# Second MLP product by Strassen's seven block products for pairs of token tiles

## The chip, the core and the metric

The kernel runs on one core of one Trainium2 chip. The time of a run is the device time of that core in microseconds. A run before the change and a run after it are compared as ratios of such times on the same chip.

## The reference, cut to what matters

```python
q_n, k_n = rmsnorm(q, g_q), rmsnorm(k, g_k)            # (8, 12, 448, 64) each
attn = softmax(q_n @ k_n.T / 8)                        # per batch and head, 448 x 448
x = (attn @ v).transpose(0, 2, 1, 3).reshape(8, 448, 768)
h = x.transpose(0, 2, 1) @ U @ V                       # mixes tokens through rank 32
u = x + h.transpose(0, 2, 1)
out = u + np.maximum(u @ w_ch1, 0.0) @ w_ch2           # 768 -> 3072 -> 768
```

Inputs and output are 32-bit floats. Attention of 12 heads gives x for each of 8 batches, a low-rank mixer over the 448 tokens gives u, and a two-layer MLP with a residual gives the output. The MLP's two products have 8 x 448 x 768 x 3072 multiplications each; they are most of the arithmetic.

## The kernel before, in words

All matmul operands are bf16, sums are 32-bit in PSUM. The 3584 tokens of the eight batches are cut into 28 tiles of 128 tokens. Since 448 is three and a half tiles, two batches share one tile: an even batch has three whole tiles and half a shared one, an odd batch the other half and three whole ones (`OFFS`, `tiles` of 3 for even and 4 for odd batches).

**Stages.** `head()` works off a hand-written word list (`HEAD`) for the attention and mixer of batch 0. Then the loop at the end of the kernel runs `mlp(b)` for b = 0 to 7, and `weave` puts the pieces of `attention(b + 1)` and `mixing(b + 1)` between the matmuls of `mlp(b)`: `mlp` is a generator which yields after six matmuls the number of columns they streamed, and `weave` takes from it until the columns done reach the share that is due to the next piece. Attention is spread over 72% of an MLP's columns and mixing over the next 13.5% (for batch 0's MLP, 58.5% and 13.5%). The schedule is manual: the order in which the Python code issues is the order on each engine, and each engine works off its own queue in that order. Semaphores are derived from the accesses to tiles.

**The MLP.** `mlp(b)` (L389) has two halves. The first product takes the batch's tiles together: for each of 24 blocks of 128 hidden columns, six matmuls with a 128 x 128 block of `w1b` as weights stream 384 (even batch) or 512 (odd batch) columns of the transposed u (tile `uA` or `uB`) into one PSUM bank `ph` (L399). ScalarE (L402) or VectorE (L404) writes its ReLU to `hT`. The second product takes tile by tile and half by half of the 768 output columns: 24 matmuls with a 128 x 128 block of `hT` as weights stream 384 columns of `w2b` into one PSUM bank `po` (L423), and VectorE adds the residual tile (L427) into `osb`, which SyncE's queue stores. That makes 28 x 2 x 24 = 1344 matmuls of 384 columns, the last 24 of them cut into 48 of 192.

**Attention.** For each pair of heads p (48 in all, `t` is two pairs): SyncE's queue loads q, k (`load`, L187) and v (`load_v`, L192; two buffers `vt`); GpSimd squares (L216), VectorE sums the squares (`reduce`, L219), ScalarE takes the inverse root (L224, L225), GpSimd scales (L230, tile `qkn`, three buffers), a DMA transposes (L263), ScalarE applies the gains (L268). From batch 2 on, at an even p both squares for two pairs of heads later are issued, and both sums at the odd p after it, so each sum stands about one pair of heads behind its squares. Scores (L281) go into banks `sc` or `sh`, ScalarE exponentiates them (L289), `products` (L296) multiplies with v, and `normalize` (L308 to L316) divides and writes x. GpSimd casts v (L202).

**Mixing.** `mix_t` and `mix_x` (L343 to L371) add the low-rank term to x in place, and `turn_u` (L373) has SyncE's queue transpose each tile to `uA` or `uB`.

**PSUM.** There are eight banks. The pool `ps_mm` has four of one bank each, which `ph`, `po`, `sh`, `o`, `pm`, `px` and `pt` take in turn; `ps_s` has two of two banks for `sc`.

## Time and profile before

| what | number |
|---|---|
| runs of the kernel before | 582.85, 584.38, 584.50 us (median 584.38) |
| the profiled execution, first to last instruction | 581.1 us |
| median of the runs less that span | 3.3 us |
| first product, matmuls of 384 and of 512 columns (L399) | 552 and 576 (24 more of 384 columns stand in `begin`, L547) |
| second product, matmuls of 384 and of 192 columns (L423) | 1320 and 48 |
| VectorE, ScalarE, GpSimd busy | 252.3, 268.5, 192.4 us |
| granted TensorE clock | 1.000 |

The page lists no time of its own for the profiled execution beside the span: what lies around the span is taken from the runs. In the profile's lines, L12 is line 12 of the kernel, PE is TensorE's matmuls, PEld its weight loads, DVE is VectorE, ACT ScalarE, POOL GpSimd and SP SyncE. A timeline line gives the start and the time from the first start to the last end, both in us, of a run of equal instructions. Matmuls overlap: the spacing from start to start, and not the duration of one, is what a matmul costs in a stream.

### The profile page before, as it was taken

To read this page: it belongs to the slowest core of one execution; us is meant where nothing else is said; L and a number is where in the kernel's file an instruction comes from. 1 tells how busy PE (TensorE), PEld (TensorE's weight loads), DVE (VectorE), ACT (ScalarE), POOL (GpSimd) and SP (SyncE) were. 2 spreads that over 40 slices of the span, in tenths; PEclk is the share of its full clock that TensorE was granted. 3 is DMA by queue.
4 is the path that set the end of the run, shared out by engine and by line. 5 is a ranking of instruction groups with operands and counts; after the bars stand their busy time and mean duration, and the time that the engine had idled before them with its cause. 6 is when DMAs were issued, how large, how long until landed. Compare 5 with 4: busy or idle time off the path is not lost.

```text
span 581.1 us, 11317 instructions
## 1 busy us (share of the span) xinstructions
PE 572.9 (99%) x4749; PEld 323.8 (56%) x4749; DVE 252.3 (43%) x565; ACT 268.5 (46%) x481; POOL 192.4 (33%) x147
## 2 busy tenths in 40 slices
PE   7999999999999999999999999999999999999997
PEld 3665665445655556545565566544565555654565
DVE  5967767233442447234152445524344152521111
ACT  6967541666306761366601874066730576112200
POOL 5956026453520553223550255405433030000000
PEclk9999999999999999999999999999999999999999
DMA  8999997845546146625154452762454310140021
GB/s 270 265 245 237 204 265 172 203 119 142 152 96 167 32 131 167 154 79 140 38 161 103 132 142 57 194 168 22 136 141 98 60 33 1 44 95 0 1 54 55
DMA packets 108275, 72.27 MB, mean 124 GB/s; under 512 B 56656, under 2 KB 104768, under 8 KB 108224
## 3 DMA queue, kind: packets, MB, share of 16 engines
q1 hardware_dynamic: 96544, 61.50, 41.2%
q0 software_dynamic: 11008, 9.44, 10.0%
q8 instruction: 37, 0.61, 0.4%
q10 hardware_dynamic: 672, 0.61, 0.4%
q14 instruction: 14, 0.11, 0.1%
HBM read 56.78 MB, written 11.01 MB: 117 GB/s over the span
## 4 chain that ended last, share of the span: by engine, by line
PE 93%; ACT 2%; DMA 2%; DVE 2%; SPq 0%; issue 0%
PE po L423 38%; PE ph L399 37%; PE o L296 7%; PE sc L281 4%; PE sh L281 3%; PE px L369 1%; ACT E L289 1%; DMA Uf<-in_moe_U_dram 1%; DMA qk<-in_k_dram 1%; PE bank L296 1%; PE sc L547 1%; ACT hT L402 1%; DVE qkn L230 1%; PE pm L343 1%; PE pt L245 0%; SPq L185 0%
## 5 line engine op out<-in xcount | busy, mean ns | idle before, releaser
L423 PE MATMUL po<-w2b,hT 128*128 128x384 bf16 (+1 forms) x1368 | 237.6, 323 | 0.0
L423 PEld LDWEIGHTS <-hT 128*128 128x128 bf16 x1368 | 128.4, 98 | 84.7 <-issue 7.0
L399 PEld LDWEIGHTS <-w1b 128*128 128x128 bf16 x1128 | 104.5, 98 | 103.1 <-issue 12.0
L230 POOL TENSOR_TENSOR qkn<-qk,rms 112x1024 bf16<-112x1024 f32 x36 | 68.4, 1901 | 221.4 <-issue 220.4
L399 PE MATMUL ph<-uB,w1b 128*128 128x512 bf16 x576 | 131.0, 379 | 0.0
L289 ACT ACTIVATE E<-sc 112x896 bf16<-112x896 f32 x138 | 123.8, 918 | 5.2 <-PE sc L281 2.5
L289 ACT ACTIVATE E<-sh 112x448 bf16<-112x448 f32 x108 | 52.8, 542 | 140.4 <-PE sh L281 140.3
L402 ACT ACTIVATE hT<-ph 128x512 bf16<-128x512 f32 (+1 forms) x122 | 66.7, 547 | 95.9 <-PE ph L399 95.7
L399 PE MATMUL ph<-uA,w1b 128*128 128x384 bf16 x552 | 98.6, 326 | 0.6 <-ACT E L289 0.5
L216 POOL TENSOR_TENSOR sq<-qk 112x1024 f32<-112x1024 f32 x42 | 78.9, 1893 | 50.8 <-DVE rec L308 23.2
L404 DVE TENSOR_SCALAR hT<-ph 128x384 bf16<-128x384 f32 (+1 forms) x66 | 41.0, 620 | 108.2 <-PE ph L399 108.0
L296 PEld LDWEIGHTS <-E 112*128 112x128 bf16 x1536 | 61.0, 98 | 15.0 <-issue 1.6
L296 PE MATMUL o<-va,E 112*128 112x65 bf16 x1344 | 56.8, 194 | 0.0
L308 DVE RECIPROCAL rec<-o 128x4 f32<-128x4 f32 x84 | 15.1, 180 | 89.5 <-PE o L296 89.1
L219 DVE TENSOR_REDUCE sums<-sq 112x16 f32<-112x1024 f32 x43 | 50.5, 1208 | 2.4 <-POOL sq L216 1.3
L281 PE MATMUL sc<-qkT 64*128 64x448 bf16 x268 | 39.3, 351 | 1.1 <-DVE qkT L252 0.8
L427 DVE TENSOR_TENSOR osb<-po,xe 128x384 f32<-128x384 f32 x32 | 17.8, 557 | 47.7 <-PE po L423 47.2
L281 PEld LDWEIGHTS <-qkT 64*128 64x128 bf16 (+1 forms) x384 | 15.5, 94 | 31.2 <-issue 19.8
L427 DVE TENSOR_TENSOR osb<-po,xo 128x384 f32<-128x384 f32 (+1 forms) x25 | 13.5, 539 | 42.3 <-PE po L423 42.3
L268 ACT ACTIVATE qkT<-qkT,gg 128x448 bf16<-128x448 bf16 x36 | 24.1, 668 | 2.7 <-DMA qkT<-qkn 2.7
L202 POOL CAST va<-vt 112x1024 bf16<-112x1024 f32 x23 | 23.9, 1041 | 1.8 <-DMA vt<-in_v_dram 1.8
L371 DVE TENSOR_TENSOR xe<-px,xe 128x384 bf16<-128x384 f32 x32 | 17.8, 555 | 15.0 <-PE px L369 10.5
(98 smaller groups left out, 262.2 us busy)
## 6 DMA issues: line engine op xcount, KB each, us to landing
qk<-in_q_dram SPq DMA_DIRECT2D x44, 256.0 KB, 4.3
qk<-in_k_dram SPq DMA_DIRECT2D x44, 256.0 KB, 4.7
vt<-in_v_dram SPq DMA_DIRECT2D x22, 512.0 KB, 5.9
w1b<-in_moe_w_ch_dram POOLq DMA_DIRECT2D x6, 768.0 KB, 21.5
w2b<-in_moe_w_ch_dram POOLq DMA_DIRECT2D x6, 768.0 KB, 34.0
out_dram<-osb SPq DMA_DIRECT2D x7, 336.0 KB, 3.4
out_dram<-osb SPq DMA_DIRECT2D x8, 288.0 KB, 2.9
out_dram<-osb SPq DMA_DIRECT2D x8, 240.0 KB, 2.8
```

The costliest lines, as they stand in the source:

```text
L216: nc.gpsimd.tensor_tensor(dst, src, src, OP.mult)
L219: nc.vector.tensor_reduce(rs_of(p, of=sums).rearrange("p (s h j) -> p s h j", s=2, h=2)[:, :, hs], sqs[p].rearrange("p (s h j d) -> p s h ...
L230: (nc.gpsimd if p >= 12 else nc.vector).tensor_tensor(qkns[p].rearrange("p j g d -> p g j d"), qk_of[t][0:SP, a].rearrange("p s h (j d) -> ...
L268: nc.scalar.activation(qT, qT, AF.Copy, scale=gg)
L281: nc.tensor.matmul(sc[hh][0:n, 0:S], flat[pp, c:c + n], blocks(p)[pp, :, 0], start=True, stop=True)
L289: nc.scalar.activation(dst, src, AF.Exp, scale=float(D) ** 0.5)
L296: nc.tensor.matmul(o[:, i, :], E[:, hh, c:c + P], va[:, hl, kc, :], start=(kc == 0), stop=(kc == NJ - 1))
L399: nc.tensor.matmul(ph, w1b[:, dc, hc * P:(hc + 1) * P], u[:, dc, :], start=(dc == 0), stop=(dc == KD - 1))
L402: nc.scalar.activation(hT[:, hc, 0:n], ph, AF.Relu)
L404: nc.vector.tensor_relu(hT[:, hc, 0:n], ph)
L423: nc.tensor.matmul(po, hT[:, hc, i * P:(i + 1) * P], w2b[:, half, hc, w0:w1], start=(hc == 0), stop=(hc == KH - 1))
L427: nc.vector.tensor_add(osb[:, cols], po, xt[i][:, cols])
```

## The change

Batch 0's three whole tiles go through both products as before (`mlp_first`, with `hT` cut to 384 columns). The shared tile 3 goes alone (`mlp_single`): 144 matmuls of 128 columns in the first product, 48 of 384 in the second. The other 24 tiles go as 12 pairs (`mlp_pair`). A pair's first product has 24 x 6 matmuls of 256 columns, two hidden blocks to a bank, with one ReLU of 512 elements for two blocks. Its second product is read as a 2 x 2 block product: the rows are the two token tiles, the inner blocks the even and the odd hidden blocks, the columns the two halves of the output. Instead of eight block products of 12 matmuls it has seven of 12 (84 matmuls of 384 columns), in Winograd's form of Strassen's scheme:

- combinations of the hidden values, for each pair of tiles: S1 and S2 on VectorE, S3 and S4 on GpSimd, each in three pieces of 128 x 512 bf16, S3 over A21 and S4 over A12 in place;
- combinations of the weights, once: T1, T2 and T4 (six pieces of 2304 elements, VectorE, in `mlp_single`), T3 over B12 in place (six pieces of 768, VectorE, in the first pair);
- three PSUM banks W, X and Y each take two products: W is read after the first by ScalarE (to `part`), X and Y by VectorE; the second product accumulates on what stands there. Z takes one;
- sums of the results: six additions from PSUM on VectorE, two in SBUF on GpSimd (384 and 768 elements wide).

For space, x lies in a ring of nine tiles `xr` and the transposed u in a ring of four `ur`; a transpose into a slot that is still to be read is held back until `have_read` is called. `opool` has two buffers for three, `qkn` two for three, `sq` one for two, `vt` one for two. So from batch 2 on the squares of pair p + 4 are issued at p and their sum at the end of the same p, and v is loaded at the odd p before its cast. Attention and mixing are woven up to named places: batch 2's attention over the single tile and the first pair's first product, and so on (`ends`).

```diff
-    opool = ctx.enter_context(tc.tile_pool(name="opool", bufs=3))
+    opool = ctx.enter_context(tc.tile_pool(name="opool", bufs=2))
...
-    hT = consts.tile([P, KH, 512], BF16, name="hT")
-    Uf = consts.tile([SP, NJ * rank], FP32, name="Uf")
-    Us = consts.tile([SP, NJ, rank], BF16, name="Us")
+    comb = consts.tile([P, 3, KH // 2, HALF], BF16, name="comb")
+    hT = consts.tile([P, KH * 384], BF16, name="hT")
+    h0 = hT.rearrange("p (k n) -> p k n", n=384)
+    h3 = hT[:, 0:KH * P].rearrange("p (k n) -> p k n", n=P)
+    hB = hT.rearrange("p (s k n) -> p s k n", s=6, n=P)
+    spare = hT.bitcast(FP32)
+    early = comb.rearrange("p s k n -> p (s k n)").bitcast(FP32)
+
+    def slot(i, n=1024):
+        return early[:, i * 1024:i * 1024 + n]
+
...
+    NX, NU = 9, 4
+    xr = consts.tile([P, NX, dm], BF16, name="xr")
+    ur = consts.tile([P, KD, NU * P], BF16, name="ur")
+    zero = xr[:, NX - 1]
...
-    vL = [consts.tile([P, HG, NJ * D], FP32, name=f"vt{i}") for i in range(2)]
+    vL = consts.tile([P, HG, NJ * D], FP32, name="vt")
+    part = consts.tile([P, HALF], FP32, name="part")
...
+        elif p < 16 and p not in sqs:
+            sqs[p] = slot(p % 4 if p > 5 else p)[0:SP]
         elif p not in sqs:
-            sqs[p] = norm.tile([SP, 2 * 2 * NJ * D], FP32, tag="sq", name="sq")
+            sqs[p] = norm.tile([SP, 2 * 2 * NJ * D], FP32, tag="sq", name="sq", bufs=1)
...
-        qkns[p] = norm.tile([SP, NJ, 4, D], BF16, tag="qkn", name="qkn", bufs=3)
+        qkns[p] = norm.tile([SP, NJ, 4, D], BF16, tag="qkn", name="qkn", bufs=2)
...
+    read, waiting = set(), []
+
+    def turn_u(t):
+        if t >= NU and t - NU not in read:
+            waiting.append(t)
+        else:
+            nc.sync.dma_start_transpose(out=u_of(t), in_=x_of(t))
+
+    def have_read(ts):
+        read.update(ts)
+        for t in [t for t in waiting if t - NU in read]:
+            waiting.remove(t)
+            turn_u(t)
...
+    def plain(po, left, half):
+        for hc in range(KH):
+            nc.tensor.matmul(po, left(hc), w2b[:, half, hc, :], start=(hc == 0), stop=(hc == KH - 1))
+            if hc % 6 == 5 and hc != KH - 1:
+                yield HALF
+
+    def mlp_single(t):
+        u = u_of(t)
+        for k in range(0, KH, 4):
+            ph = ps_mm.tile([P, 4, P], FP32, tag="mm", name="ph")
+            for j in range(4):
+                for dc in range(KD):
+                    nc.tensor.matmul(ph[:, j], w1b[:, dc, (k + j) * P:(k + j + 1) * P], u[:, dc, :],
+                                     start=(dc == 0), stop=(dc == KD - 1))
+                if j == 1:
+                    yield 2 * P
+            relu(h3[:, k:k + 4, :], ph, k % 3)
+            combine(k // 4)
+            yield 2 * P
+        have_read([t])
+        osb = new_osb()
+        for half in range(2):
+            cols = slice(half * HALF, (half + 1) * HALF)
+            po = ps_mm.tile([P, HALF], FP32, tag="mm", name="po")
+            yield from plain(po, lambda hc: h3[:, hc, :], half)
+            nc.vector.tensor_add(osb[:, cols], po, x_of(t)[:, cols])
+            yield HALF
+        put(t, osb)
...
+    w2v = w2b.rearrange("p l (k j) n -> p j l k n", j=2)
+    B11, B12, B21, B22 = w2v[:, 0, 0], w2v[:, 0, 1], w2v[:, 1, 0], w2v[:, 1, 1]
+    T1, T2, T4 = (comb[:, i] for i in range(3))
+    T3 = B12
+    A11, A21, A12, A22, S1, S2 = (hB[:, i] for i in range(6))
+    S3, S4 = A21, A12
+
+    def combine(i):
+        ks = slice(i % 2 * 6, i % 2 * 6 + 6)
+        for out, x, y in (((T1, B12, B11),), ((T2, B22, T1),), ((T4, B21, T2),))[i // 2]:
+            nc.vector.tensor_tensor(out[:, ks], x[:, ks], y[:, ks], OP.subtract)
+
+    def product(bank, left, right, start, cols=slice(0, HALF)):
+        for k in range(KH // 2):
+            nc.tensor.matmul(bank, left[:, k, :], right[:, k, cols], start=start and k == 0,
+                             stop=k == KH // 2 - 1, skip_group_check=not start)
+            if k == 5:
+                yield cols.stop - cols.start
+
+    def mlp_pair(g):
+        t0, u, last = 2 * g + 2, u_of(2 * g + 2, 2), 2 * g + 4 == 28
+        for k in range(KH // 2):
+            ph = ps_mm.tile([P, 4, P], FP32, tag="mm", name="ph")
+            for j in range(2):
+                hc, out = 2 * k + j, ph[:, 2 * j:2 * j + 2].rearrange("p a n -> p (a n)")
+                for dc in range(KD):
+                    nc.tensor.matmul(out, w1b[:, dc, hc * P:(hc + 1) * P], u[:, dc, :],
+                                     start=(dc == 0), stop=(dc == KD - 1))
+                if j == 0:
+                    yield 2 * P
+            relu(hB[:, 0:4, k, :], ph, k % 3)
+            if g == 1 and k % 2 == 0:
+                ks = slice(k, k + 2)
+                nc.vector.tensor_tensor(T3[:, ks], B22[:, ks], B12[:, ks], OP.subtract)
+            if k % 4 == 3:
+                ks = slice(k - 3, k + 1)
+                nc.vector.tensor_tensor(S1[:, ks], A21[:, ks], A22[:, ks], OP.add)
+                nc.vector.tensor_tensor(S2[:, ks], S1[:, ks], A11[:, ks], OP.subtract)
+                nc.gpsimd.tensor_tensor(S3[:, ks], A11[:, ks], A21[:, ks], OP.subtract)
+            yield 2 * P
+        have_read([t0, t0 + 1])
+        x0, x1 = x_of(t0), x_of(t0 + 1)
+        c0, c1 = slice(0, HALF), slice(HALF, dm)
+        osb0, osb1 = new_osb(), new_osb()
+
+        def bank():
+            return ps_mm.tile([P, HALF], FP32, tag="mm", name="po")
+
+        W = bank()
+        yield from product(W, A11, B11, True)
+        nc.scalar.copy(part, W)
+        yield HALF
+        Z = bank()
+        yield from product(Z, A22, T4, True)
+        nc.vector.tensor_tensor(osb1[:, c0], Z, x1[:, c0], OP.add)
+        yield HALF
+        yield from product(W, A12, B21, False)
+        nc.vector.tensor_tensor(osb0[:, c0], W, x0[:, c0], OP.add)
+        for k in range(0, KH // 2, 4):
+            ks = slice(k, k + 4)
+            nc.gpsimd.tensor_tensor(S4[:, ks], A12[:, ks], S2[:, ks], OP.subtract)
+        if last:
+            put(t0, osb0, c0)
+        yield HALF
+        X = bank()
+        yield from product(X, S2, T2, True)
+        nc.vector.tensor_tensor(osb0[:, c1], X, part, OP.add)
+        nc.gpsimd.tensor_tensor(osb0[:, c1], osb0[:, c1], x0[:, c1], OP.add)
+        yield HALF
+        Y = bank()
+        yield from product(Y, S1, T1, True)
+        nc.vector.tensor_tensor(osb1[:, c1], Y, x1[:, c1], OP.add)
+        yield HALF
+        yield from product(X, S3, T3, False)
+        nc.vector.tensor_tensor(part, X, part, OP.add)
+        both = osb1.rearrange("p (h n) -> p h n", h=2)
+        nc.gpsimd.tensor_tensor(both, both, part.rearrange("p n -> p () n").to_broadcast([P, 2, HALF]), OP.add)
+        put(t0 + 1, osb1)
+        yield HALF
+        parts = [slice(0, HALF // 2), slice(HALF // 2, HALF)] if last else [slice(0, HALF)]
+        for c in parts:
+            d = slice(HALF + c.start, HALF + c.stop)
+            yield from product(Y[:, c], S4, B22, False, c)
+            nc.vector.tensor_tensor(osb0[:, d], Y[:, c], osb0[:, d], OP.add)
+            if last:
+                put(t0, osb0, d, (nc.sync, nc.scalar))
+            yield c.stop - c.start
+        if not last:
+            put(t0, osb0)
...
-            if t + 2 < NT:
-                for a in range(2):
-                    if odd and p > 11 or p == 11 and a == 0:
-                        add(0, reduce, 2 * t + 4 + a if p > 11 else 12)
-                    elif not odd and not early:
-                        add(0, squares, 2 * t + 4 + a)
+            if p == 11:
+                add(0, reduce, 12)
+            elif t + 2 < NT and not early:
+                add(0, squares, p + 4)
...
-            if odd and p > 11 and t + 3 < NT:
-                add(0, load, t + 3)
-                add(0, load_v, t + 3)
+            if odd and p > 11:
+                if t + 3 < NT:
+                    add(0, load, t + 3)
+                if t + 2 < NT:
+                    add(0, load_v, t + 2)
             if not odd and t + 1 < NT:
                 add(0, cast_v, t + 1)
             run(p, 3)
+            if t + 2 < NT and not early:
+                add(0, reduce, p + 4)
             if early and odd and p < 11:
                 add(1, transposes, p + 1)
...
+        spans = [("first", KH * 384 + KH * HALF), ("single", KH * P + 8 * HALF)]
+        stages = [mlp_first(), mlp_single(3)]
+        for g in range(1, 13):
+            stages.append(mlp_pair(g))
+            spans += [(("ph", g), KH * 2 * P), (("po", g), 14 * HALF)]
+        begins, c = {}, 0
+        for key, n in spans:
+            begins[key] = (c, n)
...
+        ends = {2: ("po", 1), 3: ("po", 3), 4: ("ph", 5), 5: ("po", 6), 6: ("po", 8), 7: ("po", 10)}
+        for b, key in ends.items():
+            weave(fill, place(key, 0.05), attention(b))
+            weave(fill, place(key, 0.6), mixing(b))
```

## The prediction

> **What bounds the kernel now.** I read the page's first lines, then the chain of work that ended last, then the timeline of TensorE, then the groups of instructions by shape.
>
> ```profile
> span 581.1 us, 11317 instructions
> ...
> PE 572.9 (99%) x4749; PEld 323.8 (56%) x4749; DVE 252.3 (43%) x565; ACT 268.5 (46%) x481; POOL 192.4 (33%) x147
> ...
> PE   7999999999999999999999999999999999999997
> ...
> PEclk9999999999999999999999999999999999999999
> ```
>
> TensorE has work in every slice and its clock is whole (1.000 over the span). A busy PE need not be PE at its peak, so I look at spacings in the timeline (start, time from first start to last end, count):
>
> ```profile
> 25.63 0.33 PE L359 MATMUL bank<-shift,xe 128*128 128x128 bf16 x3
> ...
> 50.50 0.67 PE L296 MATMUL o<-va,E 112*128 112x65 bf16 x16
> ...
> 239.14 1.46 PE L399 MATMUL ph<-uB,w1b 128*128 128x512 bf16 x6
> ...
> 299.76 2.12 PE L423 MATMUL po<-w2b,hT 128*128 128x384 bf16 x12
> ```
>
> Take the duration of one (0.219, 0.194, 0.379, 0.326 us in the groups) off each and divide by the count less one: 55 ns for 128 columns, 32 ns for 65, 216 ns for 512, 163 ns for 384. The spacing grows with the columns, about 0.42 ns for each, and each of these matmuls loads weights of its own: weight loads hide at 32 ns. So TensorE's columns set the end, and 38% and 37% of the chain are L423 and L399, the two lines that change.
>
> Adding such spacings for all matmuls from the first ph of the loop on gives 523 us of the 539 between 38.6 and 577.9 us; the other 16 us are changes of shape (a session of scores starts some 0.1 us late and costs another 0.1) and short waits. The other engines' work hides almost wholly: the hardest stretch, the first product of batch 0's MLP (38.6 to 68.9, 30.3 us), holds 27.9 us of columns, 24.3 us of VectorE's work and 22.7 of ScalarE's by their rows.
>
> **What goes and comes on TensorE.**
>
> - Second product. Before: 1320 x 0.163 + 48 x 0.083 (192 columns: 0.163 less 192 x 0.42 ns) = 219.2 us. After: 144 (batch 0) + 48 (tile 3) + 12 x 84 = 1200, the last 12 cut in 24: 1188 x 0.163 + 24 x 0.083 = 195.6. **23.6 us go.**
> - First product. The columns stay; matmuls go from 1152 to 144 x 384, 144 x 128 and 1728 x 256. No row has 256: between 128 and 384 lies 109 ns, on the line through 384 and 512 lies 110. Before: 576 x 0.163 + 576 x 0.216 = 218.3. After: 23.5 + 7.9 + 1728 x 0.1095 = 220.6. **2.3 us come** (1.5 to 3.2 by the two ends).
>
> Net: 21.3 us less. The changed order shows all other matmuls unchanged in number.
>
> The Trainium skill speaks against the short matmuls: "TensorE: Matmul & The Clock Gate", section "Back-to-back issue gap", gives about 81 ns for each pair of weight load and matmul at 128 columns in a sustained stream. This trace has 55 ns there and 32 ns at 65 columns; by the page tile 3's first product would cost 3.7 us more.
>
> **What the other engines get.** Durations: VectorE's addition from PSUM to SBUF, 384 wide, 0.56 us (L427, L371). Its additions with both inputs bf16 in SBUF have no row. From above, the shortest 1024-wide 32-bit one with both in SBUF took 1.22 us (L230), less or plus 1.04 ns an element: 0.69 us for 512, 0.95 for 768, 2.55 for 2304. From below, a bf16 copy of 448 took 0.38 (L252), at 0.52 ns an element: 0.41, 0.55, 1.35. I take the lower ends, because the operands are 16-bit as in that copy. GpSimd by its rows (128: 0.40, 384: 0.83, 1024: 1.90): 1.05 for 512, 1.47 for 768.
>
> - VectorE: S1 and S2 72 x 0.41 = 30; T1, T2, T4 6 x 1.35 = 8; T3 6 x 0.55 = 3; 81 additions for 57, +13; x tiles that wrap in the ring, 24 more of 0.22, +5: 252 to about 311 us (340 by the upper ends).
> - GpSimd: per pair 6 x 1.05 + 0.83 + 1.47 = 8.6, x 12 = 103: 192 to 295 us.
> - ScalarE: 12 copies to `part`, 0.49 each: 268 to 274.
>
> None reaches TensorE's 550, so on the whole this is hidden. What can be seen are places:
>
> 1. **Tile 3 and the first pair's first product, with batch 2's attention.** TensorE's columns there are 41.8 us (31.6 of MLP, the rest attention and mixing); VectorE's work by its rows is 36 us at the lower ends, 47 at the upper, a share like that of the hardest stretch before (87%), but bunched: six T pieces come within 8 us of TensorE's work, and ReLUs, row sums and divisions queue behind them, whose banks TensorE then waits for. Nothing at best, 47 - 42 = 5 plus up to 8 for the port below at worst. I take 2.5, near that stretch's 30.3 - 27.9.
>
> 2. **Banks that are taken twice.** W, X and Y's second products wait for a reader of the first. Between lie 12 matmuls, 1.95 us, and attention pieces; the reader needs 0.49 to 0.56 plus what is ahead of it on ScalarE (an exponential, 0.92) or VectorE (a row sum 1.21, a division 0.76). Mostly in time. 36 such waits: 0 to 0.25 us each, 0 to 9; with batches woven through nine pairs I take 2.5. Two or three of the four banks are held then; `sh`, `o` and `px` share the rest.
>
> 3. **VectorE behind GpSimd.** The row sum of p + 4 waited for squares issued 10.5 us of TensorE's columns or more before; now 2.8 at least, 5.4 in the median, over 31 sums. GpSimd has 1.90 for the squares and up to 3.5 us ahead of them by its own list, and in three places a cast whose v was ordered only 3.5 to 6 us earlier (landing takes 5.9, behind four loads of q and k). A VectorE that stands holds ReLUs and divisions, and behind these stand banks. 0 to 0.5 us a sum, 0 to 15; I take 1.5, since backlogs reach that far in few places.
>
> 4. **The end.** The last product's two halves share bank Y; the second half waits for VectorE's 0.36 and its signals: +0.7. Before, they had two banks.
>
> On GpSimd S4 stands before the seventh product with 6.5 us of columns or more to spare for three pieces (3.2); S3 has 11. SyncE's queue: the transposes of u wait for tiles to be read, 8.5 us or more ahead of use against 2.9 for one; stores of a pair have 15 us before a buffer is asked for again. Loads issue as before, less double buffering of v. Where that cover goes, each pair would lose the excess, a microsecond or so. The head has the same words with two `qkn` buffers for three, every release issued before its next user: nothing, give or take 0.5.
>
> A row says VectorE and GpSimd get in each other's way. The shortest L230 on VectorE took 1.22 us; this one met a cast:
>
> ```profile
> 56.15 1.04 POOL L202 CAST va<-vt 112x1024 bf16<-112x1024 f32 x1 [1.01 <-DMA vt<-in_v_dram]
> ...
> 56.59 1.67 DVE L230 TENSOR_TENSOR qkn<-qk,rms 112x1024 bf16<-112x1024 f32 x1
> ```
>
> It ended 1.07 us after the cast, as if it had waited for it: +0.45. The 84 new VectorE additions with two SBUF inputs would meet GpSimd about half the time (295 of 570): 84 x 0.5 x 0.45 = 19 us on VectorE, in the bounds of places 1 and 3.
>
> The Trainium skill has this as a rule: "SBUF — State Buffer", section "Who interferes with whom", says such an instruction and a GpSimd instruction that reads SBUF exclude each other for their whole length. By it the loss per meeting could be a whole 1.90 instead of 0.45, and GpSimd's S3, issued just behind S1, could hold S2 up.
>
> **The sum.** 581.1 - 21.3 + 2.5 + 2.5 + 1.5 + 0.7 = 567.0 of span; with the 3.3 us between span and median, which I carry over, **570.3 us**.
>
> **Rivals.** A run within 0.3% of 584.4 (582.6 to 586.1) can't be told from no change.
>
> - *All of it hides*, as nearly all does now: 584.4 - 21.3 + 0.7 = 563.8. For it: shares of 87% cost little before. Against: the shortened distances.
> - *The places cost about double or triple* (2.5 + 2.5 + 1.5 becomes 13 to 19): 577 to 582.6. For it: the meetings on the port.
> - *GpSimd becomes the bound through VectorE's queue: slower.* Scales, squares, casts, S3, S4 and sums stand in one queue; at a row sum, 1.90 + 1.90 + 1.05 = 4.9 us of it against 2.8 of distance makes VectorE stand 2.1, of which a bank's slack takes about 1.2. With 31 sums at 0.9: 28 us, 570.3 - 1.5 + 28 = 597. It decides from 0.5 us a sum on, where the gain left (584.4 - 570.3 + 1.5 = 15.6) is eaten. Against it: in most places the queue is empty when squares come, and after batch 7's attention (60 us of TensorE) nothing of it is there.
> - *The gain is not there*: if 256 columns cost what a 384 does, 1728 x 0.054 = 93 us more. The rows from 65 to 512 columns lie on one line, so I give this next to nothing.
>
> **Chances.** Forecast (565 to 577) 0.60, all hides (below 565) 0.10, double or triple (577 to 582.6) 0.14, no change 0.05, slower 0.11. Faster 0.84, same 0.05, slower 0.11. The range 562 to 582 leaves out the last two and a little at each end.
>
> **What would show it.** Right: the group of 256 columns at 109 to 110 ns spacing; the 1188 of 384 columns in the second product at 163; PE in the nineties of every slice; VectorE near 311, GpSimd near 295. Place 1 shows as gaps on PE between about 90 and 140 us, place 2 as waits of PE at the product's line for ScalarE or VectorE, place 3 as VectorE's sums waiting for GpSimd's squares. The prediction fails if PE's busy share falls below some 95%, or if VectorE's additions of 512 take over 1 us.

## The result, and the profile after

The changed kernel takes 581.15 us (median of 6 runs, 580.59 to 582.42), the kernel before 584.11 beside it (6 runs, 582.46 to 584.50): ratio 0.9952, 95% interval [0.9935, 0.9968]. That is 3 us faster, where 14 were forecast. The time is above the forecast's 570.3 and just inside its range of 562 to 582. The profiled execution took 580.59 us, with a span of 578.8.

The changed kernel's page, the lines that answer to those shown of before, and the chain:

```profile
span 578.8 us, 13107 instructions
...
PE 556.6 (96%) x5457; PEld 389.6 (67%) x5457; DVE 316.0 (55%) x691; ACT 274.4 (47%) x481; POOL 319.6 (55%) x243
...
PE   7999979989999999999999999999999999999996
...
PEclk9999998989999999999999999999999999999999
...
PE 78%; DVE 8%; DMA 4%; issue 3%; ACT 3%; POOL 2%; SPq 1%; DVEq 0%; POOLq 0%
```

PE still has nearly all the span, but two of its forty slices of 14.5 us fall short (the sixth and the ninth), and so does the granted clock (in the seventh and the ninth). The loss is not spread; it has places. VectorE's share of the chain is 8% and DMA's 4%, where both had 2%; TensorE's fell from 93% to 78%.

The changed kernel's timeline of TensorE (start, time to the last end, count): the spacings are as forecast.

```profile
132.11 1.47 PE L518 MATMUL ph<-ur,w1b 128*128 128x256 bf16 x12
...
109.03 4.14 PE L475 MATMUL ph<-ur,w1b 128*128 128x128 bf16 x71
```

(1.47 - 0.273) / 11 = 0.109 us for 256 columns, (4.14 - 0.219) / 70 = 0.056 for 128. So the columns went as said: summed as in the forecast, 523.0 us before and 501.7 now, 21.3 less. The stretch from the MLP's first `ph` to its last matmul took 539.3 us before and 536.3 now (37.9 to 574.2). What it holds beyond its columns, from here on its **excess**, rose from 16.3 to 34.6 us: **18.3 of the 21.3 us were lost again**. The rest of the span's difference is at its ends: the head 0.7 us shorter, the tail 1.4 longer (4.6 after 3.2).

Cut by stages, this stretch of the changed kernel, of its experiments (below) and of its columns, in us:

| stage | columns | after | v7_own | v7_T_spread | v7_no_S | v7_no_ST |
|---|---|---|---|---|---|---|
| batch 0, first product | 27.9 | 30.4 | 30.4 | 30.4 | 30.4 | 30.4 |
| batch 0, second product | 31.1 | **37.6** | 32.2 | 32.2 | 32.2 | 32.2 |
| single tile | 20.2 | **26.3** | 26.3 | 22.2 | 23.1 | 22.2 |
| pair 1, first product | 21.6 | 24.2 | 24.2 | 24.2 | 23.7 | 23.2 |
| pair 1, second product | 16.0 | 18.3 | 18.3 | 19.8 | 16.5 | 16.5 |
| pairs 2 to 12 | 384.9 | 399.6 | 399.5 | 399.6 | 396.6 | 396.6 |
| whole stretch | 501.7 | 536.3 | 530.9 | 528.4 | 522.4 | 521.0 |

(Before, batch 0's two products took 30.3 and 31.9.) I compare stretches, not spans, since the head in front of them varied from 37.6 to 41.4 us between executions of these kernels without a change to it: in the long ones the granted clock falls back in the first 15 us (from 10 to 15 us it was 0.50 in v7_T_spread, whose head took 41.4 us, and 1.00 in the changed kernel with 37.9). Each stage time is that of one execution. Where two kernels do the same, most stages agree to 0.1 us, but the single tile has differed by 0.9 and more.

Batch 0's second product in the kernel before, and then that stage and the single tile in the changed kernel, with their busy times (after PE, PEld, DVE, ACT and POOL the granted clock, the DMA share and GB/s):

```profile
68.90:100.80 31.90, 31.90 (x298) 19.44 (x295) 21.85 (x53) 8.09 (x15) 14.23 (x8) 1.00 1.02 217
...
68.30:105.90 37.60, 33.62 (x297) 20.06 (x294) 21.68 (x53) 8.05 (x15) 12.33 (x7) 0.95 0.88 180
105.90:132.20 26.30, 23.08 (x282) 16.64 (x281) 19.84 (x25) 15.43 (x26) 18.34 (x9) 0.94 0.64 162
```

In the second row VectorE is busy for 21.68 of 37.60 us and ScalarE for 8.05: no engine is full, and yet 5.7 us more pass than before. That is a wait, not work. In the third VectorE is busy for 19.84 of 26.30, with few, long instructions (x25). And in both the clock falls: 0.05 x 37.6 and 0.06 x 26.3 are 1.9 and 1.6 us, from shares rounded to a hundredth. Cut finer, the clock was 0.50 from 87.0 to 90.3 us and 0.51 from 117.6 to 121.1, and whole again behind: two stretches of some 3.4 us, each of which loses half of that, 1.7 us.

The changed kernel's waits of TensorE (us in all, times, longest):

```profile
PE o L309 <- DVE xr L337: 3.9, 1, 3.9
PE sc L294 <- ACT E L302: 3.3, 7, 1.0
PE ph L475 <- DVE hT L421: 1.9, 1, 1.9
PE pm L360 <- DVE xr L333: 1.4, 1, 1.4
...
PE sc L294 <- ACT qkT L281: 1.3, 1, 1.3
...
PE po L506 <- DVE osb L575: 0.5, 1, 0.5
```

The second line is seven short waits of scores for ScalarE's exponentials (0.3 us in one wait before). Each other line is one wait, in one place: in batch 0's second product, the single tile, pair 1's second and its first product, and the last at the end (place 4). None is at the shared banks W, X or Y in the middle of a pair (place 2).

**The first place.** The changed kernel's timeline from 78 to 89 us, of VectorE, GpSimd and TensorE in turn:

```profile
78.52 0.06 DVE L209 MEMSET qk<- 1x4 f32 x1
86.51 0.18 DVE L324 RECIPROCAL rec<-o 128x4 f32<-128x4 f32 x1 [7.93 <-issue]
86.53 0.06 DVE L210 MEMSET vt<- 1x1 f32 x1
...
79.76 1.89 POOL L229 TENSOR_TENSOR comb<-qk 112x1024 f32<-112x1024 f32 x1 [23.39 <-DMA qk<-in_k_dram]
83.50 1.89 POOL L229 TENSOR_TENSOR comb<-qk 112x1024 f32<-112x1024 f32 x1 [1.84 <-DMA qk<-in_k_dram]
85.43 1.04 POOL L213 CAST va<-vt 112x1024 bf16<-112x1024 f32 x1
...
82.37 1.14 PE L465 MATMUL po<-w2b,hT 128*128 128x384 bf16 x6
87.38 1.06 PE L309 MATMUL o<-va,E 112*128 112x65 bf16 x16 [3.87 <-DVE xr L337]
88.25 2.11 PE L465 MATMUL po<-w2b,hT 128*128 128x384 bf16 x6
```

`touch(7)` writes one element into the slot that v of load 7 will take (L210), ahead of the load. With one v buffer this slot still holds load 6, which GpSimd casts (L213) only when two squares, each behind a transfer of k, are done, at 86.47. So an instruction of 0.06 us stands at the head of VectorE's queue for 7.93 us, with divisions behind it, their bank behind these and TensorE behind the bank. The profile puts the idle time on the instruction that happened to start first, "issue"; what held the queue is the memset beside it, as v7_own below confirms. Then the last line: six matmuls of 384 columns take 2.11 us, where they took 1.14 just before. After 3.87 us of idleness TensorE ran at half clock.

### The profile page after: what moved, and what is told of

Same layout as the page of the kernel before. It is cut to its first block, busy times and chain, and to the rows that moved or that the text cites. A ratio compares the mean times of both kernels' runs of the same rounds, so it can differ in the third digit from the quotient of the medians.

```text
span 578.8 us, 13107 instructions
## 1 busy us (share of the span) xinstructions
PE 556.6 (96%) x5457; PEld 389.6 (67%) x5457; DVE 316.0 (55%) x691; ACT 274.4 (47%) x481; POOL 319.6 (55%) x243
## 4 chain that ended last, share of the span: by engine, by line
PE 78%; DVE 8%; DMA 4%; issue 3%; ACT 3%; POOL 2%; SPq 1%; DVEq 0%; POOLq 0%
PE po L506 27%; PE ph L518 27%; PE o L309 6%; PE po L465 4%; PE sc L294 4%; PE ph L447 3%; DVE sums L232 2%; DMA vt<-in_v_dram 2%; PE sh L294 2%; DVE comb L502 1%; PE px L386 1%; ACT hT L419 1%; POOL sq L229 1%; ACT E L302 1%; DVE xr L333 1%
## 5 line engine op out<-in xcount | busy, mean ns | idle before, releaser
L518 PE MATMUL ph<-ur,w1b 128*128 128x256 bf16 x1728 | 202.3, 273 | 0.0
L518 PEld LDWEIGHTS <-w1b 128*128 128x128 bf16 x1728 | 164.1, 98 | 29.0 <-issue 9.3
L506 PEld LDWEIGHTS <-hT 128*128 128x128 bf16 x1020 | 95.5, 98 | 65.6 <-issue 7.2
L530 POOL TENSOR_TENSOR hT<-hT 128x512 bf16<-128x512 bf16 x36 | 49.3, 1370 | 122.4 <-DVE hT L528 119.0
L506 PE MATMUL po<-w2b,hT 128*128 128x384 bf16 (+1 forms) x588 | 104.6, 323 | 0.5 <-DVE osb L575 0.5
L243 POOL TENSOR_TENSOR qkn<-qk,rms 112x1024 bf16<-112x1024 f32 x36 | 69.8, 1940 | 26.4 <-ACT rms L238 19.8
L506 PE MATMUL po<-comb,hT 128*128 128x384 bf16 x432 | 78.3, 326 | 0.0
L309 PEld LDWEIGHTS <-E 112*128 112x128 bf16 x1536 | 61.9, 99 | 13.2 <-DVE xr L337 4.3
L421 DVE TENSOR_SCALAR hT<-ph 128x512 bf16<-128x512 f32 (+1 forms) x60 | 40.0, 667 | 54.3 <-PE ph L518 49.7
L552 POOL TENSOR_TENSOR hT<-hT 128x512 bf16<-128x512 bf16 x36 | 40.6, 1153 | 25.5 <-PE po L506 25.5
L229 POOL TENSOR_TENSOR comb<-qk 112x1024 f32<-112x1024 f32 x10 | 18.9, 1895 | 33.5 <-DMA qk<-in_k_dram 33.1
L465 PE MATMUL po<-w2b,hT 128*128 128x384 bf16 x192 | 37.1, 338 | 0.1
L528 DVE TENSOR_TENSOR hT<-hT 128x512 bf16<-128x512 bf16 x36 | 17.4, 483 | 36.0 <-ACT hT L419 34.7
L568 POOL TENSOR_TENSOR osb<-osb,part 128x768 f32<-128x768 f32 x12 | 21.7, 1811 | 25.1 <-DVE part L566 25.1
(122 smaller groups left out, 523.0 us busy)
```

The costliest lines, as they stand in the source:

```text
L229: nc.gpsimd.tensor_tensor(dst, src, src, OP.mult)
L243: (nc.gpsimd if p >= 12 else nc.vector).tensor_tensor(qkns[p].rearrange("p j g d -> p g j d"), qk_of[t][0:SP, a].rearrange("p s h (j d) -> ...
L309: nc.tensor.matmul(o[:, i, :], E[:, hh, c:c + P], va[:, hl, kc, :], start=(kc == 0), stop=(kc == NJ - 1))
L465: nc.tensor.matmul(po, left(hc), w2b[:, half, hc, :], start=(hc == 0), stop=(hc == KH - 1))
L506: nc.tensor.matmul(bank, left[:, k, :], right[:, k, cols], start=start and k == 0, stop=k == KH // 2 - 1, skip_group_check=not start)
L518: nc.tensor.matmul(out, w1b[:, dc, hc * P:(hc + 1) * P], u[:, dc, :], start=(dc == 0), stop=(dc == KD - 1))
```

## The experiments

Theory A: the loss sits in two early places, load 7's v and the T pieces bunched beside the single tile, each with a stretch at half clock. Theory B: every pair loses a little (shared banks, GpSimd, clock). Theory C: batch 2's attention is woven too densely over the single tile and pair 1, so ScalarE is late. Theory D: VectorE has too much to do there, however it is spread.

**v7_own** gives load 7's v a place of its own, in `comb` where nothing else lies by then; nothing else is changed.

```diff
-    v_of = {0: as_v(slot(4)), 1: as_v(slot(5)), 2: as_v(spare[:, 2048:3072]), 4: as_v(slot(4)), 5: as_v(slot(5))}
+    v_of = {0: as_v(slot(4)), 1: as_v(slot(5)), 2: as_v(spare[:, 2048:3072]), 4: as_v(slot(4)), 5: as_v(slot(5)), 7: as_v(slot(5))}
```

> The changed kernel with one edit: v of load 7 gets a place of its own (the free sixth slot) instead of the one buffer vt. Theory A: VectorE's one-element memset on vt stood 7.9 us behind GpSimd's cast of v of load 6, TensorE lost 3.9 us there and another 1.9 at half clock just after. Then the stretch from 68 to 106 us shrinks by 5 to 6 us and the time goes from 581.2 to 575 to 576.5. Rival B (the loss is a steady one: port meetings and bank waits in all pairs, or a lower clock of denser matmuls): the wait goes but the time stays above 580.

Measured: 577.18 us (575.94 to 577.82), ratio 0.9899 [0.9873, 0.9925]. Batch 0's second product falls from 37.6 to 32.2 us, all other stages stay. In v7_own's timeline of VectorE the memset now passes at once, and its row for the stage (columns as above) has PE busy throughout and the whole clock:

```profile
79.23 0.06 DVE L210 MEMSET comb<- 1x1 f32 x1
80.20 0.18 DVE L324 RECIPROCAL rec<-o 128x4 f32<-128x4 f32 x1 [0.92 <-PE o L309]
```

```profile
69.00:101.20 32.20, 32.10 (x297) 19.43 (x294) 21.68 (x53) 8.04 (x15) 12.29 (x7) 1.00 1.03 211
```

5.4 us of the 18.3 are this one memset's wait, the half clock behind it included. The time is a little above the 575 to 576.5 expected and below Theory B's 580.

**before_v7** does the reverse: the kernel before, with load 7's v in the buffer of load 6. (Load 8's v then overwrites load 7's too early; its output is not the reference's.)

```diff
-    v_of = {2: spare[:, 8 * 256:12 * 256].rearrange("p (h c) -> p h c", h=HG)}
+    v_of = {2: spare[:, 8 * 256:12 * 256].rearrange("p (h c) -> p h c", h=HG), 7: vL[0]}
```

> The kernel before with one edit: v of load 7 goes into the buffer of load 6. Theory A: the same wait as in the changed kernel now stands in this one, and it loses 4 to 6 us: 588 to 590 against 584.1. Rival B: the wait is off the path here as there: 584 to 585.

Measured: 588.51 us (587.73 to 588.97) against 582.52 of the kernel before beside it, ratio 1.0094 [1.007, 1.0119]; the one new wait of TensorE is 4.1 us for VectorE's division, as in the changed kernel, and VectorE's idle time is 8.14. So the same single line costs about 6 us in a kernel that has no Strassen at all.

**no_T** leaves T1 to T4 out; the products read plain blocks of w2.

```diff
-            combine(k // 4)
...
-    T1, T2, T4 = (comb[:, i] for i in range(3))
+    T1, T2, T4 = B12, B22, B21
...
-                nc.vector.tensor_tensor(T3[:, ks], B22[:, ks], B12[:, ks], OP.subtract)
```

> The changed kernel without the combinations of the weights: T1 to T4 are left out, and the products take the plain weight blocks in their place, so the output of the pairs is not the reference's. Theory A: the T pieces (1.3 to 3.0 us each on VectorE in the single tile's first product) hold ReLUs and banks and cost some 5 us there, with T3 another 1 in the first pair: 574 to 576. Rival C (the stretch is slow because batch 2's attention is packed too densely into it, ScalarE being the late one): 579 or more, and the single tile's stretch stays at 25 us or more.

Measured: 577.34 us (575.05 to 578.16), ratio 0.9898 [0.9866, 0.993]. The single tile falls from 26.3 to 22.6 us, pair 1's second product from 18.3 to 17.4, pairs 2 to 12 stay. The time misses Theory A's 574 to 576, but the single tile is far below Theory C's 25.

**T_spread** keeps the T pieces but cuts them into 24 of 768 elements: T1 and T2 over the single tile's two products, T4 and T3 over pair 1's.

```diff
-            combine(k // 4)
+            combine(0, k // 4)
...
+            for i, n in enumerate(plain(po, lambda hc: h3[:, hc, :], half)):
+                combine(1, 3 * half + i)
...
-                nc.vector.tensor_tensor(T3[:, ks], B22[:, ks], B12[:, ks], OP.subtract)
+                combine(2, k // 2)
...
+        def after(i):
+            if g == 1:
+                combine(3, i)
+                combine(3, i + 1)
```

> The changed kernel with the same combinations of the weights in 24 pieces of 768 elements, spread over the single tile's two products and the first pair's two, none longer than a ReLU. Theory A: VectorE's work is the same, but nothing stands 3 us or more behind it: most of what leaving T out gains comes, 575 to 578. Rival C: 580 or more. Rival D (it is VectorE's sum of work and not the bunching): at most half of what leaving T out gains.

Measured: 578.74 us (578.35 to 579.04), ratio 0.9927 [0.9899, 0.9954]. The single tile falls to 22.2 us, with a clock of 1.00, and pair 1's second product rises to 19.8. So bunching costs 4.1, of which 1.5 come back where the pieces now stand. The gain, 2.4 us of no_T's 3.8, is somewhat more than Theory D's half and less than the most of it that Theory A had.

What a bunched T piece costs stands in the changed kernel's list of VectorE's groups (busy us, mean ns of one):

```profile
L502 DVE TENSOR_TENSOR comb<-w2b,comb 128x2304 bf16<-128x2304 bf16 x4 | 7.2, 1830 | 0.0
...
L502 DVE TENSOR_TENSOR comb<-w2b 128x2304 bf16<-128x2304 bf16 x2 | 5.8, 2958 | 0.0
```

and in its timeline of the single tile (VectorE, GpSimd, then TensorE):

```profile
108.01 5.84 DVE L502 TENSOR_TENSOR comb<-w2b 128x2304 bf16<-128x2304 bf16 x2
113.78 2.18 DVE L502 TENSOR_TENSOR comb<-w2b,comb 128x2304 bf16<-128x2304 bf16 x1
115.89 0.68 DVE L421 TENSOR_SCALAR hT<-ph 128x512 bf16<-128x512 f32 x1
...
119.99 2.61 DVE L502 TENSOR_TENSOR comb<-w2b,comb 128x2304 bf16<-128x2304 bf16 x2
...
107.77 1.90 POOL L243 TENSOR_TENSOR qkn<-qk,rms 112x1024 bf16<-112x1024 f32 x1 [6.55 <-DMA qkT<-qkn]
110.62 2.02 POOL L229 TENSOR_TENSOR sq<-qk 112x1024 f32<-112x1024 f32 x1 [0.95 <-DMA qk<-in_k_dram]
112.59 2.17 POOL L213 CAST va<-vt 112x1024 bf16<-112x1024 f32 x1
...
120.14 4.21 POOL L229 TENSOR_TENSOR sq<-qk 112x1024 f32<-112x1024 f32 x1 [2.42 <-DVE sums L232]
...
116.61 1.80 PE L475 MATMUL ph<-ur,w1b 128*128 128x128 bf16 x24 [1.94 <-DVE hT L421]
118.21 2.13 PE L465 MATMUL po<-w2b,hT 128*128 128x384 bf16 x6
```

The two T4 pieces at 119.99 took 1.3 us each, the duration forecast; the first two took 2.9, beside GpSimd's scale and squares. And it goes both ways: the square at 120.14 took 4.21 us where one takes 1.90, and the cast 2.17 for 1.04. VectorE's ReLU at 115.89 stood behind three T pieces, TensorE behind the ReLU (1.94), and again six matmuls took 2.13 us for 1.14.

**v7_T_spread** has both edits. The next two start from it, and so do late, v7_no_ST and v7_no_S.

> Load 7's v has its own place again and the T pieces are spread, both at once. Theory A (two separate early losses, each with its own half-clock stretch): the gains add. Own place gave 581.15 - 577.18 = 4.0, spreading gave 581.15 - 578.74 = 2.4, so 574.8, say 574 to 576; stage of tile 2's second product near 32.2 us (37.6 in the changed kernel), single tile near 22 (26.3), first pair's second product near 19.8 (18.3, worse). Theory D (what VectorE has to do there is too much in sum, bunched or not): the losses move to the next stages, 576.5 to 578.

Measured: 575.73 us (574.03 to 576.47), ratio 0.9854 [0.9825, 0.9883]. The gains add, as Theory A says; 528.4 us of stretch. Against the columns 26.7 us of excess are left, 10.4 more than before.

**v7_T_att2** tests Theory C.

```diff
-            weave(fill, place(key, 0.05), attention(b))
-            weave(fill, place(key, 0.6), mixing(b))
+            weave(fill, place(key, 0.3 if b == 2 else 0.05), attention(b))
+            weave(fill, place(key, 0.75 if b == 2 else 0.6), mixing(b))
```

> As v7_T_spread, with batch 2's attention begun at 0.3 rather than 0.05 of its stretch and its mixing ending at 0.75 rather than 0.6. Theory C (attention stands too densely over the single tile and the first pair, so that ScalarE and VectorE are late): 1 to 2 us less than v7_T_spread, most of it in the first pair's two stages (24.2 and 18.3 in the changed kernel, against 21.6 and 16.0 of columns). Theory D: nothing within 0.5 us, the waits only move to the next stages.

Measured: 575.05 us (573.15 to 575.52), ratio 0.984 [0.9812, 0.9868]; the intervals overlap. Pair 1 gets 1.2 us shorter, pair 2 1.3 longer, the stretch is 528.6. Theory C falls: the wait only moves.

**v7_T_S_dve** moves S3 and S4 to VectorE.

```diff
-                nc.gpsimd.tensor_tensor(S3[:, ks], A11[:, ks], A21[:, ks], OP.subtract)
+                nc.vector.tensor_tensor(S3[:, ks], A11[:, ks], A21[:, ks], OP.subtract)
...
-            nc.gpsimd.tensor_tensor(S4[:, ks], A12[:, ks], S2[:, ks], OP.subtract)
+            nc.vector.tensor_tensor(S4[:, ks], A12[:, ks], S2[:, ks], OP.subtract)
```

> As v7_T_spread, with the two sums S3 and S4 (72 pieces of 1.15 to 1.37 us on GpSimd) moved to VectorE, where such a piece takes 0.4 to 0.5 us. Theory A (the steady part of the pairs is not limited by GpSimd): the same within 1 us, or up to 2 us slower where VectorE is already late early on. Rival (GpSimd's pieces and the operands they share with VectorE cost TensorE steadily): 2 to 3 us faster than v7_T_spread, seen as smaller excess in pairs 2 to 6.

Measured: 582.67 us (580.15 to 585.44), ratio 0.9974 [0.9948, 0.9999]; 8.9 us more of stretch (1.5 of it in the single tile, which the edit doesn't touch, and 6.5 in pairs 2 to 12), though GpSimd's busy time fell from 316.6 to 227.4 us and VectorE's rose only from 316.9 to 350.9. GpSimd as the limit is refuted; the numbers point to what stands in VectorE's queue. The loss is larger than I expected.

**eight** and **eight16** have eight plain products for each pair in place of seven, no S, no T, no shared bank, and load 7's v in its own place.

```diff
+        def whole(left, half, x, osb, d, parts=1):
...
+                yield from product(po, left[0], w2v[:, 0, half], True, c, stop=False)
+                yield from product(po, left[1], w2v[:, 1, half], False, c)
+                nc.vector.tensor_tensor(osb[:, o], po, x[:, o], OP.add)
...
-            spans += [(("ph", g), KH * 2 * P), (("po", g), 14 * HALF)]
+            spans += [(("ph", g), KH * 2 * P), (("po", g), 16 * HALF)]
```

The last two lines are in eight16 alone. In eight the named places still counted 14 half rows, so later batches were woven up to 20 half rows early and overwrote x before it was read; its output is not the reference's.

> Each pair's output in eight plain products of 12 matmuls in place of seven, no T, no S, with load 7's v in its own place; pairs and layout stay. Theory A: 577.2 (own place) + 12 x 2 half rows... in columns 23.4 us more, less the T pieces' 3.8 and up to 4 of waits on sums and shared banks: 592 to 597, that is the seven products are worth 15 to 20 us and the pair layout by itself costs time against the kernel before (582.5 to 584). Rival (the seven products' sums, banks and GpSimd work cost most of what their columns save, steadily over the pairs): 580 to 588.

> Eight plain products for every pair, as the run eight, but with the stretches by which attention is placed counted at eight products (16 half rows, not 14), so that attention begins where it does in the changed kernel and nothing of x is overwritten before it is read. Theory A with D: the pair layout alone, no gain from seven products. Against v7_T_spread: 23.6 us more of columns, less what S, T and shared banks cost TensorE, 3 to 8: 591 to 596. Rival (the S and T work eats most of the seven products' gain): under 588.

Measured: eight 591.04 us (589.15 to 591.39, where 592 to 597 were expected), ratio 1.0114 [1.0085, 1.0142]; eight16 587.25 (586.93 to 589.18), ratio 1.0066 [1.0041, 1.009]. So the layout by itself, without the seven products, is slower than the kernel before. I expected 591 to 596 of eight16; by its time alone the rival (under 588) would be right. By the profiled stretch, 544.6 us, it is 16.2 above v7_T_spread: of the eighth product's 144 x 0.163 = 23.5 us of columns 7.3 are eaten by what seven products bring, the upper part of my 3 to 8. (Its head and tail were 1.9 and 1.3 us shorter than v7_T_spread's.) Its excess is 544.6 - 501.7 - 23.5 = 19.4, 3.1 more than before.

**late** gives pair 1 eight plain products, without S, and spreads all T pieces over that pair; the single tile has none beside it.

```diff
+            if g == 1:
+                combine(k // 6, k % 6)
-            if k % 4 == 3:
+            elif k % 4 == 3:
...
+        if g == 1:
+            for half in (1, 0):
...
+                    yield from product(po, left[0], w2v[:, 0, half], True, stop=False)
+                    combine(which, 3 * i)
...
+                    yield from product(po, left[1], w2v[:, 1, half], False, skip=False)
...
+                    combine(which, 3 * i + 1)
+                    combine(which, 3 * i + 2)
...
+            return
```

> As v7_T_spread, but the first pair in eight plain products (no S, no T; 2.0 us more of columns) while the 24 T pieces are spread over that pair, so that VectorE has none of them beside the single tile. Theory D (what is left of the loss is VectorE's and ScalarE's sum over the single tile and the first pair, not columns): the first pair's second product was 18.4 us in the kernel with eight products everywhere against 19.8 in v7_T_spread, its first 23.2 against 24.2, so 1 to 2.5 us less, 573.2 to 574.7. Rival (a T piece costs its time wherever it stands, and the eighth product comes on top): 576 to 578.

Measured: 574.32 us (573.43 to 578.27), ratio 0.9852 [0.9824, 0.9879], the same as v7_T_spread's. Single tile and pair 1 take 66.0 us against 66.2, with 2.0 more of columns in them: the excess shrinks by what the eighth product costs. By its time alone it lies in Theory D's 573.2 to 574.7, but the ratio to the kernel before, measured beside each, shows no gain: neither theory clearly. Its profiled execution was the longest of the six, and shows why; see the last section.

**v7_no_ST** and **v7_no_S** settle what the 7.3 us are. They are v7_T_spread with the seven products' matmuls and final additions in place, but no S and T, or no S.

```diff
-                nc.vector.tensor_tensor(S1[:, ks], A21[:, ks], A22[:, ks], OP.add)
-                nc.vector.tensor_tensor(S2[:, ks], S1[:, ks], A11[:, ks], OP.subtract)
-                nc.gpsimd.tensor_tensor(S3[:, ks], A11[:, ks], A21[:, ks], OP.subtract)
...
-            nc.gpsimd.tensor_tensor(S4[:, ks], A12[:, ks], S2[:, ks], OP.subtract)
...
+    S1, S2, S3, S4 = A22, A11, A21, A12
```

> As v7_T_spread, with the seven products' matmuls and their additions at the end in place, but the sums S1 to S4 and T1 to T4 left out (the products read plain blocks instead, so the pairs' outputs are not the reference's). The stretch of the MLP was 528.4 us with seven products and 544.6 with eight, where columns say 23.6 apart: 7.4 us go to something that seven products bring. Theory D (it is VectorE's and GpSimd's work on the sums): 7.4 us come back, 567 to 570, the first pair's second product near 16.5. Rival (it is the shared banks and the order of the seven products): 574 to 576, nothing comes back.

> As v7_T_spread with the T pieces kept and only S1 to S4 left out (the pairs' outputs are not the reference's). Theory D, cost where the T pieces meet the first pair's S: most of it in the first pair, so 1 to 3 us of the 7.4 come back here, 573 to 575. If instead the S sums cost TensorE steadily in every pair: 5 to 7 come back, 569 to 571.

Measured: v7_no_ST 566.02 us (565.11 to 568.75), ratio 0.9716 [0.9689, 0.9743]; v7_no_S 568.76 (566.41 to 569.68), ratio 0.9746 [0.9718, 0.9775]. The stretch without both is 521.0: 7.4 us come back, and its excess, 19.3, is that of eight16. Nor do the stages show the shared banks: of the second products of pairs 1 to 11, nine take the same in v7_no_ST as in eight16 without the eighth product, to 0.02 us; pair 9's takes 0.07 more, and pair 5's 0.7 less, behind a first product that takes 0.8 more. So the shared banks cost nothing that can be seen, and the sums cost it all: S 6.0 us (528.4 - 522.4), T where it is spread 1.4 (522.4 - 521.0). S costs 3.0 us over pairs 2 to 12, in seven stages by 0.2 to 0.6 us each and in the others nothing, and 3.8 in pair 1, where the T pieces still are. The single tile, which has no S, was 0.9 longer in v7_no_S's execution; without that S would be 6.9 and T 0.5. I expected 1 to 3 from S with T, or 5 to 7 if every pair paid alike; it is 6.0 to 6.9, and more than half of it is pair 1.

Pair 1's second product in v7_T_spread, VectorE and GpSimd:

```profile
150.41 1.22 DVE L232 TENSOR_REDUCE sums<-sq 112x16 f32<-112x1024 f32 x1 [0.81 <-POOL sq L229]
152.76 0.42 DVE L529 TENSOR_TENSOR hT<-hT 128x512 bf16<-128x512 bf16 x1 [1.14 <-ACT hT L419]
...
153.56 0.17 DVE L324 RECIPROCAL rec<-o 128x4 f32<-128x4 f32 x1
...
157.93 1.97 DVE L504 TENSOR_TENSOR w2b<-w2b 128x768 bf16<-128x768 bf16 x2
...
161.22 1.69 DVE L504 TENSOR_TENSOR w2b<-w2b 128x768 bf16<-128x768 bf16 x2
...
144.64 1.39 POOL L531 TENSOR_TENSOR hT<-hT 128x512 bf16<-128x512 bf16 x1 [2.91 <-DVE hT L529]
...
148.17 2.20 POOL L229 TENSOR_TENSOR sq<-qk 112x1024 f32<-112x1024 f32 x1
...
158.31 3.71 POOL L561 TENSOR_TENSOR hT<-hT 128x512 bf16<-128x512 bf16 x3 [3.65 <-PE po L508]
```

and what TensorE waited for there:

```profile
154.78 0.57 PE L360 MATMUL pm<-xr,Ub 128*32 128x384 bf16 x4 [1.38 <-DVE xr L333]
...
160.42 1.14 PE L508 MATMUL po<-comb,hT 128*128 128x384 bf16 x6 [0.57 <-DVE xr L388]
```

The same place in v7_no_S, VectorE:

```profile
151.10 0.18 DVE L324 RECIPROCAL rec<-o 128x4 f32<-128x4 f32 x1 [0.73 <-PE o L309]
...
155.05 1.02 DVE L504 TENSOR_TENSOR w2b<-w2b 128x768 bf16<-128x768 bf16 x2
```

Three things are to be seen. The row sum at 150.41 waits 0.81 us for GpSimd's squares, which stand behind S3 (L531, 144.64) and a scale; this is the wait that the forecast's place 3 named. S1 (L529) then waits 1.14 us for ScalarE's ReLU at the head of VectorE's queue, and the division at 153.56 stands behind it; without S the division waits for nothing but its own matmuls. And two T3 pieces take 1.97 and 1.69 us while GpSimd has S4, 1.02 without S4. How the 3.8 us divide among the three was not tried.

## Why the prediction was right in part and wrong in its sum

Right: the columns (21.3 less, at 109 ns for 256 and 56 for 128), that what they save can be lost again only in places, S1 and S2 (0.41 us forecast, 0.48 and 0.43 measured), VectorE's total (311 forecast, 316.0; GpSimd's came to 319.6, not 295), the kind of loss in place 1, place 4, and the sign. Of the rivals, the one in which the places cost double or triple held the time (577 to 582.6), and part of its reason, the meetings with GpSimd, was right. That it held the time is in part luck: by the table below places 1 to 3 cost 9.9 us for 6.5, one and a half times, and the rest came from two terms that it doesn't name. GpSimd did not become the bound.

The terms, forecast and measured in the stretch:

| term | forecast | measured | from |
|---|---|---|---|
| columns | -21.3 | -21.3 | spacings of after |
| one v buffer | 0 | +5.4 | after less v7_own |
| place 1, T pieces bunched | +2.5 | +2.5 | v7_own less v7_T_spread |
| T pieces, spread | (in place 1) | +1.4 | v7_no_S less v7_no_ST |
| S sums | (in places 1 and 3) +1.5 | +6.0 | v7_T_spread less v7_no_S |
| place 2, shared banks | +2.5 | 0 | second products of v7_no_ST and eight16 |
| place 4, the end | +0.7 | +0.7 | pair 12's second product: v7_no_ST's 14.5 less eight16's 15.8 without the eighth product's 2.0 |
| layout | 0 | +2.3 | excess of v7_no_ST less before's, 3.0, less place 4 |
| sum | -14.1 | -3.0 | |

Outside the stretch the tail is 1.4 us longer, with the other tile's 336 KB of store issued beside the last halves; in eight16, where that store goes out before the last four products, the tail is 3.2 us as before. And the 3.3 us that the forecast carried over set the median of the runs against the span of a faster execution: the changed kernel's executions took 1.8 us more than their own spans, so the sum was 1.5 us too high there.

**The step that failed most** is "Loads issue as before, less double buffering of v. Where that cover goes, each pair would lose the excess, a microsecond or so." It was put at nothing in the sum, and priced as a late transfer. What ran late was no transfer: the slot's release stood in VectorE's queue as a one-element memset, behind a cast, behind squares, behind loads. What place 3 did for the row sums, to ask what is queued behind a waiting instruction, was not done for `touch`. It costs 5.4 us once, at load 7, not a little in each pair.

**The second** is the S sums, for which places 1 and 3 had 1.5 us. Place 3 watched VectorE's row sums wait for GpSimd's squares: these waits came to 2.0 us in 4 places, none over 0.8. In pair 1 of v7_T_spread one such wait stands in the chain of the loss, 0.81 us. The longer wait that the change adds, S1 for ScalarE's ReLU, was not named; the page's list of VectorE's waits in the changed kernel shows it:

```profile
DVE hT L528 <- ACT hT L419: 34.7, 22, 3.7
...
DVE sums L232 <- POOL sq L229: 2.0, 4, 0.8
```

34.7 us in 22 waits, most of them in a slack that costs nothing (the stages that agree with and without S), but in pair 1 with a division behind. S was to be nearly hidden, and took 6.0 us.

**Third**, place 1 was taken near its lower end: 2.5 of 0 to 13. Its stages, the single tile and pair 1's first product, took 50.5 us in the changed kernel and 45.4 in v7_no_ST, so T and S cost 5.1 there, twice the term; that bunching alone also measures 2.5 is chance. With pair 1's second product it is 68.8 against 61.9, 6.9 us. The durations behind the choice held for a T piece alone (1.34 us), not for one beside GpSimd (2.9). The forecast saw this meeting and priced it at 0.45 us; here a pair of T pieces lost about 3.

**Fourth**, place 2 was oversized, by all of its 2.5 us: pair 11's two products, with no attention beside them, took 15.7 and 13.6 us, their columns to the tenth.

**What no term had**: TensorE's idle time is not paid once. In the changed kernel some 3.4 us of the loss in the two bad stages, 1.7 in each, is half clock behind the stalls. The Trainium skill says this in "TensorE: Matmul & The Clock Gate", section "Part 1: The HAM clock gate": after an idle window of about 3.4 us the array runs at half its clock until it has been busy for as long. The trace agrees on the half (2.11 us for 1.14) and on how long it lasts (87.0 to 90.3 us), but not on the idleness: here a wait of 1.94 us was enough, and in v7_own one of 2.00 (twelve matmuls then took 3.79 us where they take 2.1). Not every wait of nearly that length is followed by it: behind one of 1.8 us in v7_T_S_dve, and behind the changed kernel's 1.4, the clock stayed whole.

Open: the layout's 2.3 us. eight16 and v7_no_ST show that they are there without any sum and without shared banks; which part of the new layout they are (the rings, the ReLUs of 512, the 256-column groups), no run tells apart. The list of waits gives a hint: TensorE's scores wait for ScalarE's exponentials for 2.3 us in v7_no_ST and 2.5 in eight16, against 0.3 before. Nor was it tried what the other store at the end costs by itself; eight16's tail only points to it.

The changed kernel's gain comes to little, then, because the sums S and T and one buffer were paid in VectorE's queue, and a part in the layout. The best of these kernels that compute the whole reference are v7_T_att2, late and v7_T_spread, at 0.984, 0.9852 and 0.9854 of the kernel before, which the intervals don't tell apart; v7_no_ST's 0.9716 shows what seven products would be worth if their sums cost nothing.

## What to carry to other kernels

When a buffer goes from two to one, look for the instruction that releases it, on which engine's queue it stands, and what it would wait for; a store of one element can cost 5 us. For every instruction that a change adds to a shared queue, name its latest input, not only its duration. And once the bound engine is full, price a stall of it of some two microseconds or more as the stall and a stretch at half clock behind it, here up to 1.7 us more.

## What the runs showed of the hardware

VectorE and GpSimd can shut each other out for much longer than the 0.45 us that the forecast saw. In late's profiled execution two squares and a cast stood back to back on GpSimd just as VectorE began a scale (VectorE, GpSimd, TensorE):

```profile
50.30 5.63 DVE L243 TENSOR_TENSOR qkn<-qk,rms 112x1024 bf16<-112x1024 f32 x1
...
50.11 3.75 POOL L229 TENSOR_TENSOR comb<-qk 112x1024 f32<-112x1024 f32 x2
53.80 1.04 POOL L213 CAST va<-comb 112x1024 bf16<-112x1024 f32 x1
...
56.71 3.70 PE L447 MATMUL ph<-ur,w1b 128*128 128x384 bf16 x12 [3.20 <-DVE xr L337]
```

The scale took 5.63 us, where the other scales of this line took 1.22, and ended 1.1 us after the cast: it got through only when GpSimd's three instructions were over. TensorE stood 3.20 us and then took 3.70 for twelve matmuls that take 2.1, so that batch 0's first product took 35.3 us in place of 30.4. In v7_T_spread's execution the same two squares stood apart (49.11 and 54.95), and that stage took 30.4. The execution with the meeting took 578.27 us, the median of late's runs is 574.32. The rule of the Trainium skill that the forecast weighed and set aside ("SBUF — State Buffer", section "Who interferes with whom": the two exclude each other for the whole instruction) is what this trace shows; between several instructions in a row VectorE did not get in either, in this one execution.

GpSimd's additions of 512 bf16 elements took 1.37 us (S3) and 1.15 (S4), against 1.05 forecast from 32-bit rows.
